# Attention and routed experts: a pair's loads in eight transfers behind exponentials, a batch's rows stored together

## The chip, the cores and the metric

The kernel runs on one core of a Trainium2 chip. The metric is the device time of one execution in microseconds (us): the median of three timed runs. The profile is of one further execution.

## The reference

Inputs are q, k, v of 8 batches, 8 heads, 576 positions and 64 values a head, and the weights of 8 experts. Cut to what matters:

```python
q_rot, k_rot = rotate(q), rotate(k)                  # x1*cos - x2*sin, x1*sin + x2*cos
scores = matmul(q_rot, k_rot.T) / sqrt(64)
attn = softmax(scores)
x = matmul(attn, v)                                  # -> 4608 tokens of 512 values
e_idx = argmax(x @ w_gate)                           # one expert per token
gate = softmax(x @ w_gate)[e_idx] * sigmoid(x @ w_output_gate)[e_idx]
out = gate * (relu(x @ w1[e_idx]) @ w2[e_idx])
```

## The kernel before

**The tiling.** Two heads make a pair, so there are 4 pairs a batch and 32 in all. A pair's scores are computed in nine units of 128 x 576 (128 rows of one head, and one unit of what is left of both). The schedule is counted in steps, nine to a pair, one for each unit: `step` (L367) writes the instructions of a unit, or of two units at a time, and behind them whatever is listed for the step. `PREPARED`, `EVENTS` and `PREP` (L45 to L59) list (name, step relative to the pair's first, order within the step). The program is unrolled and has one order of instructions for each engine; an engine, and SP's queue of transfers too, takes its instructions in that order, and each waits for the data that it needs.

**A unit.** TensorE computes the scores (`sc`, L521); VectorE copies them out and takes their extreme (`pm`, L530); ScalarE takes the exponential with the sum of a row (L537, `exp` at L532); VectorE transposes blocks of 32 (`pt`, L543 and L545); and in the following pair's steps TensorE multiplies with v (`acc`, L567, `values` at L556), in 18 blocks of 32 keys, eight small matmuls each (four row groups by two heads). Then ScalarE evicts (`ac`, L574 to L576), TensorE turns the result back (L582), and VectorE divides by the sums into `xb` (L594).

**Preparation.** A pair needs q and k, each with a copy whose halves are swapped: four planes of 128 x 576 in the tile `raw` (two buffers). `load` (L452) brings them in two transfers of 576 KB on SP's queue: k's two planes at step -18, q's at step -15. POOL multiplies with the table of cosines and sines (L472), k first, adds (L476), ScalarE rounds to the high part (L482), POOL subtracts to get the low part (`kq`, L485). In POOL's order the next pair's k multiplication stands just ahead of this pair's low part. `loadv` (L458) brings v in two transfers of 576 KB, one a head, at steps 5 and 7 of the pair itself, into `v` (two buffers). None of these transfers waits for anything but its buffer: a load of q and k can go as soon as POOL has finished the pair two ahead, a load of v as soon as the values of the pair two ahead have been read.

**Ranking and storing.** After a batch's last pair, `place` (L607) lists the work of choosing experts, numbering tokens and storing the batch's rows of `xb` to memory, mostly on POOL, over the following pairs. A token's gate factor is copied into the rows by `gated` (L690) and the rows leave by `store` (L697), three transfers of 640, 640 and 160 KB on SP's queue. For the first six batches L812 lists them: columns 0 and 1 gated at 29, the first store at 33, the rest gated at 38, the other stores at 42 (in steps, counted from 20 steps behind the batch's last pair's start). The last two batches go another way.

**The experts.** When all of attention's steps are written, `body` (L221 to L231) lists the first weight loads (`wr`, L1098) on the same queue; ScalarE and VectorE split weights in two parts (L1107, L1109), and TensorE multiplies (L1142, L1150, L1192).

Of the kernel before, what the change touches and what calls it, by code (L numbers as in the profile page):

```python
# [14 lines left out]
AF = mybir.ActivationFunctionType  # L15
# [12 lines left out]
NCH = 5  # L28
# [13 lines left out]

NB, TAIL, PE_ = S // 32, 160, 192

PREPARED = [("load1", -18, 1), ("load0", -15, 1), ("mult1", -14, 1), ("mult0", -11, 1), ("add", -9, 1), ("hi", -6, 1), ("lo", -5, 2)]  # L45
EVENTS = [
    ("lasts", 1, 2), ("loadv0", 5, 2), ("loadv1", 7, 2),
    ("av0", 12, 1), ("av1", 13, 0), ("av2", 14, 0), ("av3", 16, 0),
    ("den0", 10, 2), ("den1", 15, 2), ("den2", 15, 3), ("evict", 16, 1), ("newxb", 18, 1), ("back", 19, 1), ("divide", 19, 2),
]  # L50
# [3 lines left out]
PREP = {  # L54
# [5 lines left out]
}  # L60

PIECES = ((0, 5), (5, 7), (7, 12), (12, 18))
# [69 lines left out]
class Small:  # L132


    def __init__(self, p):
        self.p, self.tag = p, "sc"
# [139 lines left out]
class Attention:  # L276


    def __init__(self, tc, nb, pools, cc, ident, ii, first, trib, oneb, cnt, zero, qk, v, xd, row, lists):
        nc = tc.nc  # L280
        px, px2, pa2, pp1, pp2, ps_s, small, ps_a = pools
        NT = nb * S
        own = []
        self.tops = px.tile([P, NCH, E + 1], F32, name="score"), px.tile([P, NCH + 1, E], BF16, name="hot")
        self.inits = [lambda t=t, x=x: nc.gpsimd.memset(t, x) for t, x in zip(self.tops, (0.5, 0.0))]

        def init(bd, z, rz, ac):
            nc.gpsimd.memset(ac[:, NCH - 1, :, :], 0.0)
            nc.gpsimd.tensor_copy(bd.rearrange("p a b -> p (a b)"), zero)
            nc.gpsimd.memset(z, 1.0)  # L290
            nc.gpsimd.memset(rz, 1.0)

        for i in range(2):
            o = (px.tile([P, 2, P], F32R, name=f"bd{i}"), px.tile([P, 2 * NCH], F32, name=f"z{i}"),
                 px.tile([P, 2 * NCH], F32, name=f"rz{i}"), pa2.tile([P, NCH, 4, 32], F32, tag=f"ac{i}", name=f"ac{i}", bufs=1))
            self.inits.append(lambda o=o: init(*o))
            own.append(o)
        npair = nb * NP
        self.G, self.pairs = 9 * npair, []
        raw0, rt = first  # L300
        for n in range(npair):
            self.pairs.append(Pair(tc, pools, n, own[n % 2], ident, ii, rt, qk[n // NP, n % NP], v[n // NP, n % NP]))
        self.pairs[0].raw = raw0

        self.todo = {}
        self.last, self.later = [], []
        at = self.at
        xbs = {}

        def newxb(b):  # L310
            xbs[b] = px2.tile([P, NCH, XW], F32, tag="xb", name=f"xb{b}")

        for i, pr in enumerate(self.pairs):
            g, b = 9 * i, i // NP
            fs = {"lasts": pr.lasts, "den0": pr.den0, "den1": pr.den1, "den2": pr.den2, "evict": pr.evict, "back": pr.back,
                  "newxb": lambda pr=pr, b=b: newxb(b) if pr.hp == 0 else None}
            fs["divide"] = lambda pr=pr, b=b: pr.divide(xbs[b])
            for t, n in ((slice(0, 1), "0"), (slice(1, 2), "1"), (slice(0, 2), "")):
                fs[f"mult{n}"] = lambda pr=pr, t=t: pr.mult("P", t)
                fs[f"add{n}"] = lambda pr=pr, t=t: pr.add("P", t)  # L320
                fs[f"hi{n}"] = lambda pr=pr, t=t: pr.high(t)
                fs[f"lo{n}"] = lambda pr=pr, t=t: pr.low("P", t)
            for t in range(2):
                fs[f"load{t}"] = lambda pr=pr, t=t: pr.load(t)
                fs[f"loadv{t}"] = lambda pr=pr, t=t: pr.loadv(t)
            for k, (b0, b1) in enumerate(PIECES):
                fs[f"av{k}"] = lambda pr=pr, b0=b0, b1=b1: [pr.values(j) for j in range(b0, b1)]
            for name, o, k in [*PREP.get(i, PREPARED), *EVENTS]:
                at(g + o, k, fs[name])
            if i % NP == NP - 1:  # L330
                fs = place(tc, (px, px2, small), self.pairs, b, NT, cc, trib, oneb, cnt, xbs, xd, row, lists, self.tops, self.later)
                if b == nb - 1:
                    self.last = fs
                else:
                    for k, p, f in fs:
                        at(g + PLACE + k, p, f)
# [5 lines left out]
    def at(self, g, k, f):  # L342
        self.todo.setdefault((g, k), []).append(f)
# [10 lines left out]
    def start(self, consts):  # L354
        at = self.at
        for f in self.inits:
            f()

        self.pairs[1].load(1)
        self.pairs[1].load(0)  # L360
        self.pairs[0].start()
        self.todo.setdefault((0, 0), []).insert(0, self.pairs[0].started)
        for g, f in consts:
            at(g, 2, f)
        self.rest(lambda g: g < 0)
# [36 lines left out]
class Pair:  # L402
# [46 lines left out]
    def eng(self, eng):  # L449
        return self.nc.gpsimd if eng == "P" else self.nc.vector  # L450

    def load(self, t):  # L452

        if t:
            self.raw = self.pp2.tile([P, 4, S], F32, tag="raw", name=f"raw{self.nm}")
        self.nc.sync.dma_start(out=self.raw[:, 2 * t:2 * t + 2, :], in_=self.qkd[:, 2 * t:2 * t + 2, :])

    def loadv(self, t):  # L458

        if t == 0:  # L460
            self.v = self.pa.tile([P, 2, NB, D], F32, tag="v", name=f"v{self.nm}")
        self.nc.sync.dma_start(out=self.v[:, t, :, :], in_=self.vd[:, t, :, :])


    def sides(self, a, t, s, x):
# [26 lines left out]
            self.nc.scalar.copy(self.bd[r, :, r], self.kq.bitcast(F32)[r, 0:2, QM:S])  # L492

    def begin(self):
        self.pc, self.ps, self.m = {}, {}, {}

        self.pt = self.pa.tile([P, 9, S], F32, tag="pt", name=f"pt{self.nm}")

# [33 lines left out]
    def exp(self, i):  # L532
        zi = 8
        if self.STEPS[i]:
            c, h = self.STEPS[i]
            zi = 2 * c + h
        self.nc.scalar.activation(self.pc[i], self.pc[i], AF.Exp, bias=self.m[i], scale=-1.0, accum_out=self.z[:, zi:zi + 1])  # L537

    def turn(self, units):

# [66 lines left out]
def place(tc, pools, pairs, b, NT, cc, trib, oneb, cnt, xbs, xd, row, lists, tops, later):  # L607
# [82 lines left out]
    def gated(c0, c1):  # L690

        V.tensor_copy(xbs[b][:, c0:c1, P], T["eg"][:, c0:c1])
# [115 lines left out]
    if b == NT // S - 2:  # L808
        later += [lambda i=i: store(i) for i in range(3)]
        fs += [(22, 2, s13)]  # L810
    else:
        fs += [(29, 2, lambda: gated(0, 2)), (33, 2, lambda: store(0)), (38, 2, lambda: gated(2, NCH)),  # L812
               (42, 2, lambda: store(1)), (42, 2, lambda: store(2))]
    return fs


# [523 lines left out]
```

## Time and profile before

| | us |
|---|---|
| median of 3 runs (961.87 to 965.65) | 965.22 |
| the profiled execution | 961.01 |
| its span, from first to last instruction | 959.2 |
| TensorE (PE) busy | 911.8 (95%) |
| VectorE (DVE) busy | 753.4 (79%) |
| ScalarE (ACT) busy | 658.7 (69%) |
| GpSimd (POOL) busy | 528.9 (55%) |

The span is the profiled execution's instructions; its own time has 1.8 us around it. PE is the matmuls and PEld the weight loads that overlap them. Attention takes the first half of the span, the experts the second. TensorE's granted clock is at full speed in all slices.

### The profile page before, as it was taken

Reading aid. Unit: us, or ns where it says so; the run is one execution under the profiler, and the core shown is the slowest. Engines: PE = TensorE matmul, PEld = TensorE weight load, DVE = VectorE, ACT = ScalarE, POOL = GpSimd, SP = SyncE. Lnnn points to the kernel's source line nnn. Section 1 sums busy time; section 2 is a strip of 40 time slices with the busy share of each in tenths; the row PEclk is TensorE's granted clock in tenths of the full one; section 3 lists DMA queues with packets and bytes.
Section 4 is the critical chain, followed back from the end, with each engine's and each line's share of the span. In section 5 each row is a group of like instructions: output and inputs, shape, how many; then the busy total and the mean of one; then the engine's idle time right before and its main releaser. Section 6 shows DMA issues by size and latency. Waiting matters only on the chain.

```text
span 959.2 us, 34178 instructions
## 1 busy us (share of the span) xinstructions
PE 911.8 (95%) x14445; PEld 789.2 (82%) x14445; DVE 753.4 (79%) x1354; ACT 658.7 (69%) x1373; POOL 528.9 (55%) x483
## 2 busy tenths in 40 slices
PE   4999999999999989989899999999999999999997
PEld 3777777878878777777788998999899998999986
DVE  6899999999999989989588776657765757668562
ACT  4777789899998988797764544457645656556562
POOL 5898898898989898797222222142514315042140
PEclk9999999999999999999999999999999999999999
DMA  6554466365636555554299867667876868768560
GB/s 239 199 180 147 178 227 231 142 227 200 245 135 243 203 182 182 177 186 173 97 359 313 304 205 239 219 217 270 290 269 226 292 199 303 255 225 289 198 203 25
DMA packets 57821, 208.42 MB, mean 217 GB/s; under 512 B 7818, under 2 KB 8252, under 8 KB 57664
## 3 DMA queue, kind: packets, MB, share of 16 engines
q1 hardware_dynamic: 49920, 183.78, 54.8%
q0 software_dynamic: 6464, 21.26, 5.9%
q8 instruction: 115, 1.88, 0.8%
q10 hardware_dynamic: 1280, 1.15, 0.4%
q14 instruction: 42, 0.34, 0.1%
HBM read 186.09 MB, written 22.43 MB: 217 GB/s over the span
## 4 chain that ended last, share of the span: by engine, by line
PE 69%; DVE 13%; issue 6%; POOL 5%; ACT 5%; DMA 2%; POOLq 0%; DVEq 0%; SPq 0%; ACTq 0%
PE py L1192 20%; PE ph L1150 19%; PE acc L567 12%; PE sc L521 10%; DVE pm L530 6%; PE ph L1142 3%; DVE pt L545 2%; ACT pm L537 2%; PE acc L582 2%; POOL raw L472 2%; DVE pt L543 2%; PE mtp L1115 2%; POOL kq L485 1%; DVE xb L594 1%; DMA out<-y,2idx 1%
## 5 line engine op out<-in xcount | busy, mean ns | idle before, releaser
L537 ACT ACTIVATE pm<-pm,m 128x576 f32<-128x576 f32 x288 | 221.7, 770 | 55.9 <-DVE pm L530 52.6
L1109 DVE TENSOR_TENSOR wl<-wr,wh 128x1024 fp32r<-128x1024 f32 x172 | 216.2, 1271 | 37.2 <-ACT wh L1107 34.2
L530 DVE TENSOR_SCALAR_CACHE_REDUCE pm<-sc 128x576 f32<-128x576 f32 x288 | 205.1, 744 | 24.4 <-PE sc L521 19.4
L567 PE MATMUL acc<-pt,v 32*64 32x128 f32 (+1 forms) x9216 | 198.5, 295 | 21.2 <-issue 9.2
L1192 PE MATMUL py<-wh,ht 128*128 128x512 f32 x640 | 214.0, 400 | 0.0
L1150 PE MATMUL ph<-xt,wh 128*128 128x256 f32 x1088 | 198.3, 284 | 0.0
L567 PEld LDWEIGHTS acc<-pt,v 32*64 32x64 f32 x9216 | 157.5, 131 | 47.6 <-issue 29.7
L1107 ACT CAST wh<-wr 128x1024 fp32r<-128x1024 f32 x184 | 187.8, 1049 | 0.0
L521 PE MATMUL sc<-kq 64*128 64x288 f32 x1536 | 159.8, 320 | 15.4 <-ACT kq L482 9.6
L1150 PEld LDWEIGHTS ph<-xt,wh 128*128 128x128 f32 x1088 | 169.8, 190 | 2.6 <-DVE xt L1131 1.2
L472 POOL TENSOR_TENSOR raw<-raw,rt 128x1152 f32<-128x1152 f32 x62 | 164.8, 2658 | 0.0
L521 PEld LDWEIGHTS sc<-kq 64*128 64x128 f32 x1536 | 121.5, 190 | 48.7 <-issue 20.8
L1150 PE MATMUL ph<-xt,wl 128*128 128x256 f32 x544 | 154.0, 283 | 0.0
L1192 PEld LDWEIGHTS py<-wh,ht 128*128 128x128 f32 x640 | 120.3, 188 | 25.2
L1192 PE MATMUL py<-wl,ht 128*128 128x512 f32 x320 | 125.8, 393 | 0.0
L543 DVE STREAM_TRANSPOSE pt<-pm 128x576 f32<-128x576 f32 x160 | 116.7, 759 | 2.1 <-ACT pm L537 2.1
L1166 ACT ACTIVATE ht<-ph 128x512 fp32r<-128x512 f32 x68 | 40.7, 598 | 112.9 <-PE ph L1150 103.3
L1197 POOL DMA_INDIRECT out<-y,2idx x24 | 26.0, 1083 | 166.1 <-ACT y L1206 104.7
L1167 DVE SCALAR_TENSOR_TENSOR ht<-ph,ht 128x512 fp32r<-128x512 f32 x68 | 47.0, 691 | 73.7 <-ACT ht L1166 70.3
L1150 PEld LDWEIGHTS ph<-xt,wl 128*128 128x128 f32 x544 | 103.0, 189 | 0.2 <-DVE wl L1109 0.2
L545 DVE STREAM_TRANSPOSE pt<-pm 128x1152 f32<-128x1152 f32 x64 | 87.9, 1373 | 0.7 <-ACT pm L537 0.7
L485 POOL TENSOR_TENSOR kq<-raw,kq 128x1152 fp32r<-128x1152 f32 (+1 forms) x33 | 82.8, 2509 | 8.7 <-ACT kq L482 8.5
(243 smaller groups left out, 1105.0 us busy)
## 6 DMA issues: line engine op xcount, KB each, us to landing
wr<-in_w SPq DMA_DIRECT2D x184, 512.0 KB, 4.4
raw<-in_qk SPq DMA_DIRECT2D x64, 576.0 KB, 5.2
v<-in_v SPq DMA_DIRECT2D x64, 576.0 KB, 6.1
xd<-xb SPq DMA_DIRECT2D x16, 640.0 KB
xd<-xb SPq DMA_DIRECT2D x8, 160.0 KB, 5.1
rt<-in_rope ACTq DMA_DIRECT2D x1, 576.0 KB
xg<-xd,2idx POOLq DMA_INDIRECT x24, 6.7
out<-y,2idx POOLq DMA_INDIRECT x24, 3.4
```

The source lines that it names most:

```text
L472: self.eng(eng).tensor_tensor(out=rv, in0=rv, in1=rt, op=ALU.mult)
L485: self.eng(eng).tensor_tensor(out=self.sides(self.kq, t, 0, x), in0=self.sides(self.raw, t, 0, x), in1=self.sides(self.kq.bitcast(F32), t, ...
L521: self.nc.tensor.matmul(self.ps[i][:, a, :HS], st, self.kq[r, mov, x], start=(n == 0), stop=(n == 2))
L530: self.nc.vector.tensor_scalar(self.halves(i), self.ps[i][:, :, :HS], 1.0, FAR, op0=ALU.mult, op1=ALU.min, accum_out=self.m[i])
L537: self.nc.scalar.activation(self.pc[i], self.pc[i], AF.Exp, bias=self.m[i], scale=-1.0, accum_out=self.z[:, zi:zi + 1])
L543: self.nc.vector.transpose(out=self.pt[:, c + 5 * h, :], in_=self.pc[units[0]])
L545: self.nc.vector.transpose(out=self.pt[:, c:c + 6:5, :], in_=self.pc[units])
L567: nc.tensor.matmul(self.acc[h * D:h * D + D, a, o:o + 32 * n], self.v[r, h, j, :], self.pt[r, u:u + n, 32 * j:32 * j + 32], start=(j == 0) ...
L1107: self.nc.scalar.copy(wh, r)
L1109: eng.tensor_tensor(out=wl, in0=r, in1=wh.bitcast(F32), op=ALU.subtract)
L1150: nc.tensor.matmul(ph[:, f, :], st[:, dc, fs], mv[:, dc, :], start=(n == 0), stop=(n == 11))
L1192: self.nc.tensor.matmul(py[h], st[:, f, hs], mv, start=(f == 0 and n == 0), stop=(f == 7 and n == 2))
```

## The change

Each of q's and k's four planes gets a transfer of its own (288 KB), at steps -18 to -15, in the order k, k swapped, q, q swapped; v is loaded in four quarters at steps 4 to 7. Each transfer is made dependent on the exponential of one unit: q and k of a pair on those of units 0 to 3 of the pair two ahead, v on those of units 4 to 7 of the same pair. Pair 1's loads, at the program's start, depend on none. For the first six batches the gate factors are copied at once at 24, and all three stores are listed at 33.

```diff
-PREPARED = [("load1", -18, 1), ("load0", -15, 1), ("mult1", -14, 1), ("mult0", -11, 1), ("add", -9, 1), ("hi", -6, 1), ("lo", -5, 2)]
+LOADED = [(f"load{t}", t - 18, 2) for t in range(4)]
+
+PREPARED = [*LOADED, ("mult1", -14, 1), ("mult0", -11, 1), ("add", -9, 1), ("hi", -6, 1), ("lo", -5, 2)]
 EVENTS = [
-    ("lasts", 1, 2), ("loadv0", 5, 2), ("loadv1", 7, 2),
+    ("lasts", 1, 2), *[(f"loadv{t}", t + 4, 2) for t in range(4)],
...
-            for t in range(2):
-                fs[f"load{t}"] = lambda pr=pr, t=t: pr.load(t)
-                fs[f"loadv{t}"] = lambda pr=pr, t=t: pr.loadv(t)
+            for t in range(4):
+                fs[f"load{t}"] = lambda i=i, pr=pr, t=t: pr.load(t, self.pairs[i - 2].ex[t])
+                fs[f"loadv{t}"] = lambda pr=pr, t=t: pr.loadv(t, pr.ex[t + 4])
...
-        self.pairs[1].load(1)
-        self.pairs[1].load(0)
+        for t in range(4):
+            self.pairs[1].load(t)
...
-    def load(self, t):
-
-        if t:
+    def behind(self, dma, ex):
+
+        if ex is not None:
+            info = mybir.DependencyInfo(mybir.DependencyClass.Sync, mybir.DependencyReason.DATA)
+            self.tc.add_manual_dep(dma.ins, ex.ins.name, info, reason="transfers evenly in time")
+
+    def load(self, t, ex=None):
+
+        if t == 0:
             self.raw = self.pp2.tile([P, 4, S], F32, tag="raw", name=f"raw{self.nm}")
-        self.nc.sync.dma_start(out=self.raw[:, 2 * t:2 * t + 2, :], in_=self.qkd[:, 2 * t:2 * t + 2, :])
-
-    def loadv(self, t):
+        t ^= 2
+        self.behind(self.nc.sync.dma_start(out=self.raw[:, t, :], in_=self.qkd[:, t, :]), ex)
+
+    def loadv(self, t, ex):
 
         if t == 0:
             self.v = self.pa.tile([P, 2, NB, D], F32, tag="v", name=f"v{self.nm}")
-        self.nc.sync.dma_start(out=self.v[:, t, :, :], in_=self.vd[:, t, :, :])
+        h, j = t // 2, slice(t % 2 * 9, t % 2 * 9 + 9)
+        self.behind(self.nc.sync.dma_start(out=self.v[:, h, j, :], in_=self.vd[:, h, j, :]), ex)
...
-        self.nc.scalar.activation(self.pc[i], self.pc[i], AF.Exp, bias=self.m[i], scale=-1.0, accum_out=self.z[:, zi:zi + 1])
+        self.ex[i] = self.nc.scalar.activation(self.pc[i], self.pc[i], AF.Exp, bias=self.m[i], scale=-1.0, accum_out=self.z[:, zi:zi + 1])
...
-        fs += [(29, 2, lambda: gated(0, 2)), (33, 2, lambda: store(0)), (38, 2, lambda: gated(2, NCH)),
-               (42, 2, lambda: store(1)), (42, 2, lambda: store(2))]
+        fs += [(24, 2, s13), (33, 2, lambda: store(0)), (33, 2, lambda: store(1)), (33, 2, lambda: store(2))]
```

The same `LOADED` takes the place of the two loads in `PREP`'s lists for pairs 2 and 3.

## Rows read from the trace of the kernel before

**Rows 1.** The page: busy us (share), instructions by engine; a queue: packets, MB, share

```profile
PE 911.8 (95%) x14445; PEld 789.2 (82%) x14445; DVE 753.4 (79%) x1354; ACT 658.7 (69%) x1373; POOL 528.9 (55%) x483
...
q8 instruction: 115, 1.88, 0.8%
```

**Rows 2.** Stretch of attention: length, busy time by engine, PEclk, DMA share, GB/s

```profile
core 0: us, PE busy (x) PEld busy (x) DVE busy (x) ACT busy (x) POOL busy (x), PEclk, DMA share, GB/s
13.30:472.80 459.50, 428.33 (x11323) 353.19 (x11322) 428.13 (x888) 386.81 (x1000) 394.90 (x372) 1.00 0.54 191
```

**Rows 3.** The chain of waits through one pair: start us, us, what

```profile
82.79 1.41 DVE pm L530 x4
...
96.18 1.40 DVE pm L530 x3
```

**Rows 4.** Timeline of SP's queue: start us, us of issue, transfer

```profile
340.31 1.81 SPq L456 DMA_DIRECT2D raw<-in_qk  x2
342.22 0.85 SPq L462 DMA_DIRECT2D v<-in_v  x2
...
351.27 0.38 SPq L700 DMA_DIRECT2D xd<-xb  x1
353.88 0.92 SPq L456 DMA_DIRECT2D raw<-in_qk  x2
357.98 0.81 SPq L462 DMA_DIRECT2D v<-in_v  x2
...
447.99 65.19 SPq L1098 DMA_DIRECT2D wr<-in_w  x25
```

**Rows 5.** Timeline of PEld: start us, us, operation, count [idle before <- releaser]

```profile
144.44 0.43 PEld L521 LDWEIGHTS sc<-kq 64*128 64x128 f32 x5 [0.77 <-issue]
...
351.80 1.02 PEld L567 LDWEIGHTS acc<-pt,v 32*64 32x64 f32 x56 [1.15 <-issue]
353.05 0.82 PEld L521 LDWEIGHTS sc<-kq 64*128 64x128 f32 x12 [0.23 <-issue]
354.04 1.04 PEld L567 LDWEIGHTS acc<-pt,v 32*64 32x64 f32 x60 [0.17 <-issue]
356.92 0.74 PEld L567 LDWEIGHTS acc<-pt,v 32*64 32x64 f32 x36 [1.84 <-issue]
...
372.50 0.20 PEld L567 LDWEIGHTS acc<-pt,v 32*64 32x64 f32 x5 [1.53 <-issue]
...
412.99 1.30 PEld L567 LDWEIGHTS acc<-pt,v 32*64 32x64 f32 x73 [1.72 <-issue]
...
417.55 1.01 PEld L567 LDWEIGHTS acc<-pt,v 32*64 32x64 f32 x53 [1.31 <-issue]
```

**Rows 6.** Stretches of a burst of loads and of a wait (columns as in rows 2)

```profile
69.00:71.00 2.00, 1.92 (x18) 1.51 (x14) 2.00 (x6) 1.96 (x7) 2.00 (x2) 1.00 1.00 385
...
348.00:351.00 3.00, 2.86 (x69) 1.96 (x68) 2.76 (x5) 2.94 (x7) 3.00 (x2) 1.00 0.36 137
351.00:352.00 1.00, 0.20 (x11) 0.20 (x19) 1.00 (x5) 1.00 (x2) 1.00 (x3) 1.00 0.00 0
```

**Rows 7.** Line 567: waits in the weight loads' queue, ns min/median/max

```profile
L567 PEldq EVENT_SEMAPHORE  x33: 51/51/1509, 28.3 to 461.4; - x33
```

**Rows 8.** Timeline of ACT: the end of unit 1's exponential in pair 14

```profile
208.36 0.19 ACT L537 ACTIVATION_READ_ACCUMULATOR pm<-pm,m 128x1 f32 x1
```

**Rows 9.** Timeline of POOL: pair 16's k multiplication, pair 15's low part

```profile
208.70 2.66 POOL L472 TENSOR_TENSOR raw<-raw,rt 128x1152 f32<-128x1152 f32 x1
...
212.06 2.65 POOL L485 TENSOR_TENSOR kq<-raw,kq 128x1152 fp32r<-128x1152 f32 x1
```

**Rows 10.** Timeline of PEld: pair 15's first scores

```profile
217.64 0.83 PEld L521 LDWEIGHTS sc<-kq 64*128 64x128 f32 x12 [0.22 <-issue]
```

**Rows 11.** Tile wr: its 512 KB loads from issue to landing

```profile
DMA to landing us min/median/max: 3.4/4.4/7.2
```

**Rows 12.** Timeline of ACT: unit 7 of the last pair, the first split of weights

```profile
460.02 0.19 ACT L537 ACTIVATION_READ_ACCUMULATOR pm<-pm,m 128x1 f32 x1
...
468.33 2.95 ACT L1107 CAST wh<-wr 128x1024 fp32r<-128x1024 f32 x3
```

More of the change, by code (lines that the diff above doesn't have):

```diff
@@ L56 @@
     1: (("mult1", -9, 1), ("add1", -9, 1), ("mult0", -8, 1), ("add0", -7, 1), ("hi1", -5, 1), ("lo1", -4, 1), ("hi0", -3, 1), ("lo0", -2, 1)),
[1 row of a table removed]
+    2: (*LOADED, ("mult1", -11, 1), ("add1", -10, 1), ("mult0", -9, 1), ("add0", -7, 1), ("hi1", -6, 1),
         ("lo1", -5, 1), ("hi0", -4, 1), ("lo0", -3, 1)),
[1 row of a table removed]
+    3: (*LOADED, ("mult1", -11, 1), ("mult0", -9, 1), ("add", -7, 1), ("hi", -4, 1), ("lo", -4, 2)),
 }
@@ L494, in begin @@
     def begin(self):
-        self.pc, self.ps, self.m = {}, {}, {}
+        self.pc, self.ps, self.m, self.ex = {}, {}, {}, {}
         self.pt = self.pa.tile([P, 9, S], F32, tag="pt", name=f"pt{self.nm}")
```

2 rows, old and new, of the table PREP are left out of this document.

## The prediction

> **What bounds the kernel now.** I began with the stretches. Attention runs from 13.3 to 472.8 us, and in it TensorE (428.3 us) and VectorE (428.1 us) are busy for equal shares of 459.5 us [rows 2]: neither has room. The change edits only loads and stores of this half; the experts behind it stream weights through code that it leaves alone. The chain of waits then shows what a quiet pair costs: its last scores are read by VectorE at 82.79 and those of the next pair at 96.18, so 13.39 us a pair, by matmuls and VectorE work that follow on each other without a gap [rows 3]. 32 such pairs would take 428 us; the stage is about 30 us longer, part of it the batches' own ranking work and the start.
>
> Next I looked for where a pair is longer. SP's queue shows it: the loads of v are issued as soon as a pair's values have been read, and from 342.22 to 357.98 they stand 15.76 us apart instead of 13.39 [rows 4]. The weight-load rows of those stretches show why. Before the loads at 351.80, 356.92, 372.50, 412.99 and 417.55 TensorE sat idle for 1.15, 1.84, 1.53, 1.72 and 1.31 us, and for 0.77 us before 144.44, each time "issue", that is, no other engine was waited for; the same change of line costs 0.16 to 0.23 us elsewhere, as at 353.05 and 354.04 [rows 5].
>
> What is missing there is the program itself. From the idle time at 351.80 to the one at 356.92 lie 56 + 12 + 60 = 128 weight loads [rows 5], and as many matmuls. The page counts 14445 of each, 28890 in all, and 115 packets of kind "instruction" with 1.88 MB, 16 KB each: 251 instructions a packet [rows 1]. So the two waits are one packet apart, at its edges: TensorE had run dry before its next block came. And the block came late behind loads. Two transfers of q and k at 340.31 and two of v at 342.22, 576 KB each, keep the transfer engines moving until about 350; in 351 to 352 they move nothing at all (share 0.00) while TensorE still waits [rows 4, 6]. The block thus passed no earlier than the end of the burst. The next wait follows a 640 KB store at 351.27 and two loads at 353.88 [rows 4].
>
> **The change, part by part.** (1) Loads. A pair's four transfers of 576 KB become eight of 288 KB, each allowed only after one exponential: q and k behind units 0 to 3 two pairs ahead, v behind units 4 to 7 of the pair itself. A transfer of 288 KB takes 0.77 us at the 385 GB/s of a burst [rows 6], and units are 13.39 / 9 = 1.5 us apart, so no queue builds up. The six waits lose all but the ordinary 0.2 us: 0.57 + 0.95 + 1.64 + 1.33 + 1.52 + 1.11 = **-7.1 us**. They lie on TensorE in a stage without slack, so I count them whole. The Trainium skill, Runtime: NRT & Kernel Launch, Instruction fetch mechanics, says that the engine fetches its next block of 256 instructions while it executes the current one, at a cost that is mostly hidden. The trace agrees on the size of the block, not on the cost, which is 7.1 us here; by that sentence this term would be about 0 and the sum 4 us above the time before.
>
> (2) What is late next: transfers are now under way in every phase of a pair, 8 x 0.77 / 13.39 = 46% of the time, also where TensorE goes through a block fastest (128 weight loads from 351.80 to about 355.1, in 3.3 us [rows 5]). A block behind one slice waits 0.77 / 2 = 0.38 us on average. One such block in each of 28 pairs gives at most 28 x 0.46 x 0.38 = 4.9 us, at least 0. I take **+1.5**, nearer to zero, because most bursts of before, three times as deep, were survived: only six waits stand out.
>
> (3) The gate on POOL. POOL multiplies the k half as soon as it is there, and the previous pair's low part (L485), which that pair's scores need, stands behind this multiplication in POOL's order. Today nothing gates it: in the tightest kind of pair, one a batch, it starts at 208.70 and the low part at 212.06 [rows 9]. After the change the second slice waits for unit 1, whose exponential is read out at 208.36 + 0.19 = 208.55 [rows 8]. From issue to landing no row shows 288 KB; 512 KB take 3.4 / 4.4 / 7.2 us (least, median, most) [rows 11], less the 0.6 us of the missing bytes 2.8 / 3.8 / 6.6. I take 3.0, near the least, since little else is then in flight: ready at 211.55, the low part done at 211.55 + 2.66 + 0.70 (two small steps between them) + 2.65 = 217.56, and the scores start at 217.64 [rows 9, 10]. That fits by 0.08 us. Bounds for 7 batches: 0, and 7 x 0.7 = 5 us at 3.8. I take **+0.5**. What POOL loses there it has back in its later waits for ScalarE.
>
> (4) SP's queue. Everything in it now stands behind exponentials, the stores and the first weights too. The last v slice waits for unit 7 of the last pair, read out at 460.2 [rows 12], so the first weights, issued at 447.99 today [rows 4], go after 461. They are first read at 468.33, three in 2.95 us [rows 12]; landing in 4.4 us makes some 465.6 for the first [rows 11], and 1.36 us more for each of the following. It fits, but TensorE's blocks then meet a denser burst than before. Bounds 0 and 4 us (first weights landing 7.2 us after issue, and one more late block); I take **+0.8**.
>
> (5) Stores. Six batches store 640 + 640 + 160 KB at the end of one pair, not over two. Gating in one POOL copy instead of two saves some 0.2 us of POOL; the factors are then ready. The stores are 3.8 us of transfers at 385 GB/s [rows 6] in front of the next pair's first slices, which land about 1 us later, and POOL's multiplication with them. Bounds 0 and 6 x 0.5; I take **+1.0**. The store's buffer is free a pair earlier; no row shows a wait for it today, so that brings nothing.
>
> (6) Finer tiles need about two more waits of TensorE's queue per pair, at 51 ns a piece [rows 7]: 32 x 2 x 0.051 = 3.3 us at most, 0 at least. The queue runs ahead of the array, so **+0.3**.
>
> Sum: -7.1 + 1.5 + 0.5 + 0.8 + 1.0 + 0.3 = -3.0 us. The profiled execution took 961.0 us (span 959.2), so 958.0. It is the fastest one shown; the median, 965.22, is 4.2 us above it. Late blocks are a matter of phase and the likeliest thing to differ between executions of one program, so I let half of the 4.2 go as well: 958.0 + 2.1, about **960 us**, 0.54% under the median.
>
> **The rivals.** *Given back* (0.20): the long waits vanish and short ones take their place in each pair, as in (2) at its upper bound, with (6) at 1.3. That is -7.1 + 4.9 + 0.5 + 0.8 + 1.0 + 1.3 = +1.4 against the profile's 961.0; with half of the 4.2 us, 964.5. For it speaks that a fast block has only 3.3 us [rows 5]; against it, that bursts three times as deep rarely hurt.
>
> *Nothing hangs on the bursts* (0.12): the late blocks have another cause, and time stays at 965. The position after whole bursts [rows 4, 6] speaks against it. The Trainium skill, DMA: Bandwidth & Descriptors, Queues, rings and completion order, has each engine go round between its queues packet by packet; by that a block would never wait for a burst to drain, and spreading the loads would bring nothing. The trace disagrees: at 351 to 352 the burst had drained and TensorE still stood.
>
> *POOL gate, the slower side* (0.18): slices land later than 3.0 us after issue, because the refills or the stores are in front of them. Each us beyond costs a us in each of 7 batches, on TensorE itself. It decides from about 3.5 us, where 7 x 0.42 eats the 3 us won. At the median-like 3.8, together with the stores' 1 us, the scores wait 1.7 us a batch: 7 x 1.7 = 12, in place of the 1.5 of (3) and (5), so 970.5. For it: a margin of 0.08 us. Against: in most other pairs POOL multiplies later by itself.
>
> **How the numbers follow.** Main case 0.50, from 953 to 963 as the bounds of (2) to (6) make it; some 0.44 of it lies under 960.4. Within 0.5% (4.8 us, about what a measurement of this kernel can tell from no change) lie the rest of it, 0.06, and the two middle rivals, 0.32: 0.38. Slower by more than that: 0.18. The range runs from 952 to 970; left out are the worse half of the gate's cases and a larger gain.
>
> **What would show it.** Right: SP's rows have one load per 1.5 us; idle times of over 0.8 us before values (L567) are gone between 340 and 420; v loads stay about 13.4 us apart there. (2) is wrong if there are many new "issue" waits of 0.3 to 0.8 us. The gate shows as TensorE's scores waiting for POOL L485, and the raw load as POOL's releaser. (4) shows as ScalarE L1107 waiting for weights near 468. The forecast falls if waits of over 1 us stay although no burst is left, or if scores wait for POOL in most pairs.

## The result and the profile after

The changed kernel took **975.04 us** (median of 4 runs, 971.85 to 978.39), the kernel before 963.55 beside it (4 runs, 957.19 to 965.65): 1.0136 times as long, 95% interval 1.0107 to 1.0166. Here and below, the ratio and its interval are worked out from the fast runs and need not equal the quotient of the two medians. It is slower by more than the range allowed. The profiled execution took 974.82 us, its span is 973.0.

The page of the changed kernel. First the busy times and the refills of the instruction queue, which answer to [rows 1], then POOL's multiplication (busy, mean ns | idle before it and what ended it), and the issues (KB each, median us from issue to landing):

```profile
PE 921.5 (95%) x14445; PEld 795.9 (82%) x14445; DVE 755.0 (78%) x1354; ACT 659.4 (68%) x1373; POOL 529.5 (54%) x477
...
q8 instruction: 115, 1.88, 0.8%
...
L482 POOL TENSOR_TENSOR raw<-raw,rt 128x1152 f32<-128x1152 f32 x62 | 164.4, 2653 | 31.9 <-DMA raw<-in_qk 31.9
...
raw<-in_qk SPq DMA_DIRECT2D x124, 288.0 KB, 3.0
```

and the multiplication's line in the page of the kernel before:

```profile
L472 POOL TENSOR_TENSOR raw<-raw,rt 128x1152 f32<-128x1152 f32 x62 | 164.8, 2658 | 0.0
```

The programs are equally long (115 refills, the same instructions on TensorE). What is new is 31.9 us in which POOL stands in front of its multiplications and waits for q and k; before, that number was 0.0. The landing of 3.0 us that the prediction took is the true median of these 124 transfers. It is not what the pairs behind the stores got.

**Where the time lies.** ScalarE's rows give the place of the last pair's unit 7, to be laid beside 460.02 in [rows 12]; the two earlier ones are unit 0 and unit 1 of the pair shown further down.

```profile
196.70 0.19 ACT L547 ACTIVATION_READ_ACCUMULATOR pm<-pm,m 128x1 f32 x1
...
197.46 0.19 ACT L547 ACTIVATION_READ_ACCUMULATOR pm<-pm,m 128x1 f32 x1
...
472.48 0.19 ACT L547 ACTIVATION_READ_ACCUMULATOR pm<-pm,m 128x1 f32 x1
```

Attention up to there is 472.48 - 460.02 = 12.5 us longer; the rest of the span grew from 499.2 to 500.5 us, by 1.3. TensorE's lines up to that point say in what. Before (busy us, mean ns | idle before them, and what ended it):

```profile
L567 PE MATMUL acc<-pt,v 32*64 32x160 f32 (+1 forms) x8928 | 192.0, 295 | 18.5 <-DVE xb L594 8.0 <-issue 6.5 <-ACT rc L720 3.9
L521 PE MATMUL sc<-kq 64*128 64x288 f32 x1524 | 157.8, 319 | 5.8 <-DVE pm L530 3.5 <-issue 1.0 <-POOL kq L485 0.6
L582 PE MATMUL acc<-ii,ac 128*128 128x160 f32 x300 | 48.8, 309 | 1.5 <-ACT ac L576 0.2
```

and after:

```profile
L577 PE MATMUL acc<-pt,v 32*64 32x128 f32 (+1 forms) x8928 | 192.4, 295 | 13.8 <-DVE xb L604 7.1 <-ACT rc L730 4.0 <-issue 2.3
L531 PE MATMUL sc<-kq 64*128 64x288 f32 x1524 | 163.7, 322 | 11.9 <-POOL kq L495 6.0 <-DVE pm L540 4.3 <-issue 0.6
L592 PE MATMUL acc<-ii,ac 128*128 128x160 f32 x300 | 52.3, 324 | 2.3 <-ACT ac L586 1.5
```

The late instruction blocks did go: "issue" in front of the values fell from 6.5 to 2.3 us. In their place scores wait for POOL's low part: 6.0 us, where it was 0.6. And the same matmuls take longer: 5.9 us more for the scores, 3.5 for the turning back. In all, TensorE up to that point is busy 10.2 us longer (429.6 in place of 419.3 us) and idle 2.2 us longer. The waits of attention with its end (0 to 490 us; total, times, longest) complete the picture:

```profile
POOL raw L482 <- DMA raw<-in_qk: 31.9, 17, 4.5
...
DVE pm L540 <- PE sc L531: 26.3, 34, 2.8
...
PEld sc L531 <- POOL kq L495: 7.5, 7, 2.0
```

VectorE, as full as TensorE, waits for scores 26.3 us in place of 19.4.

**One batch of it.** SP's queue, at the end of the first pair behind a batch:

```profile
193.90 0.90 SPq L710 DMA_DIRECT2D xd<-xb  x2
194.85 1.40 SPq L712 DMA_DIRECT2D xd<-xb  x1
196.95 3.32 SPq L465 DMA_DIRECT2D raw<-in_qk  x4
```

The three stores go just ahead of the four slices. The first slice leaves as soon as unit 0 is read out (196.70 + 0.19), the second behind unit 1 (197.46 + 0.19 = 197.65). The stretches there (columns as in [rows 2]), and, below them, three stretches to come back to:

```profile
194.00:196.00 2.00, 1.95 (x18) 1.56 (x14) 2.00 (x6) 1.93 (x7) 1.92 (x2) 1.00 0.82 182
196.00:198.00 2.00, 1.55 (x42) 1.29 (x45) 2.00 (x3) 1.99 (x8) 1.58 (x2) 1.00 0.98 386
198.00:200.00 2.00, 2.00 (x75) 1.71 (x57) 2.00 (x5) 1.98 (x6) 1.28 (x3) 1.00 1.03 387
200.00:202.00 2.00, 2.00 (x46) 1.51 (x44) 1.88 (x4) 1.83 (x4) 0.00 (x0) 1.00 0.96 346
202.00:203.60 1.60, 1.60 (x83) 1.34 (x80) 1.56 (x5) 1.23 (x3) 0.00 (x0) 1.00 0.96 324
...
324.30:327.70 3.40, 3.40 (x16) 3.07 (x18) 2.67 (x6) 2.34 (x8) 3.32 (x2) 0.50 0.21 40
382.30:385.70 3.40, 3.40 (x17) 3.12 (x18) 1.84 (x5) 2.42 (x7) 3.32 (x3) 0.50 0.00 1
430.10:433.50 3.40, 3.40 (x16) 3.07 (x17) 2.33 (x6) 3.33 (x11) 3.40 (x2) 0.50 0.89 331
```

The engines are full from 196 to 203.6. From 194 on they move 364 + 772 + 774 + 692 + 518 = 3.1 MB (GB/s times us, slice by slice), which is more than the stores (1.47 MB) and all four slices (1.18 MB) together. So k's second slice was complete when nearly everything issued around it had been moved, and not after the stores' rest alone. The chain of waits and POOL's timeline show when (idle before in brackets):

```profile
197.69 5.84 DMA raw<-in_qk
...
203.66 2.65 POOL L482 TENSOR_TENSOR raw<-raw,rt 128x1152 f32<-128x1152 f32 x1 [4.23 <-DMA raw<-in_qk]
206.26 2.64 POOL L495 TENSOR_TENSOR kq<-raw,kq 128x1152 fp32r<-128x1152 f32 x1
```

and TensorE's weight loads who pays:

```profile
208.96 0.70 PEld L531 LDWEIGHTS sc<-kq 64*128 64x128 f32 x10 [2.03 <-POOL kq L495]
```

The chain has one link of 5.84 us from unit 1 to the multiplication; in two more batches the same link is 5.12 us (at 312.70) and 6.01 us (at 370.82). In [rows 9] the low part stands right behind this multiplication; here the multiplication comes 4.23 us after POOL was ready.

**The clock.** In the three stretches listed last TensorE's granted clock is 0.50, its lower level of 1.2 GHz. Before, no stretch of attention up to the last pair was below full speed. Behind the last pair both kernels have one such stretch (the changed one from 481.3); the page's 40 slices are too coarse to show the one of the kernel before:

```profile
472.90:476.30 3.40, 3.40 (x16) 3.40 (x17) 0.15 (x2) 1.17 (x5) 0.00 (x0) 0.50 0.02 5
```

TensorE's rows at the first of the changed kernel's three, and the same ten matmuls of the last pair:

```profile
323.27 0.92 PE L531 MATMUL sc<-kq 64*128 64x288 f32 x10 [1.64 <-POOL kq L495]
324.12 2.93 PE L592 MATMUL acc<-ii,ac 128*128 128x160 f32 x10
...
473.56 1.62 PE L592 MATMUL acc<-ii,ac 128*128 128x160 f32 x10 [1.04 <-ACT ac L586]
```

It stood idle for 1.64 us, waiting for POOL, computed for about 1 us, and then ten matmuls that take 1.62 us at 473.56 took 2.93. The second stretch follows a wait for POOL too (0.95 us, at 382.26). The third does not: it follows 1.24 us of waiting for ScalarE's eviction (at 429.88), and experiment 5, whose scores are on time, has the same 1.24 us with the lower clock behind it (at 415.37). Nor does every wait bring the lower clock: the one of 2.03 us at 208.96 did not. Three times 3.4 us at half the clock is work of 5.1 us at full clock: 5.1 us lost, half of the 10.2 us by which TensorE's busy time grew up to 472.67. Of the 5.1 us, the 3.4 of two stretches go with the late scores. The Trainium skill, TensorE: Matmul & The Clock Gate, HAM oscillation, describes this: waits for transfers between pieces of work make the engine start the next piece at the lower clock. The trace agrees in kind, though its waits of 0.95 to 1.64 us are shorter than those of the section's example. The other half of the growth can't be assigned: the ends of matmuls are modelled.

### The profile page after: what moved, and what is told of

Its sections match the earlier page's. It is cut to its first block, busy times and chain, and to the rows that moved or that the text cites. A ratio compares the mean times of both kernels' runs of the same rounds, so it can differ in the third digit from the quotient of the medians.

```text
span 973.0 us, 34540 instructions
## 1 busy us (share of the span) xinstructions
PE 921.5 (95%) x14445; PEld 795.9 (82%) x14445; DVE 755.0 (78%) x1354; ACT 659.4 (68%) x1373; POOL 529.5 (54%) x477
## 4 chain that ended last, share of the span: by engine, by line
PE 68%; DVE 12%; ACT 7%; issue 5%; POOL 4%; DMA 4%; POOLq 0%; DVEq 0%; ACTq 0%
PE py L1201 21%; PE ph L1159 19%; PE acc L577 11%; PE sc L531 9%; DVE pm L540 6%; ACT pm L547 3%; PE ph L1151 3%; DMA raw<-in_qk 2%; PE acc L592 2%; DVE pt L555 2%; PE mtp L1124 2%; POOL kq L495 2%; DVE pt L553 2%; POOL raw L482 2%; DVE xb L604 1%
## 5 line engine op out<-in xcount | busy, mean ns | idle before, releaser
L540 DVE TENSOR_SCALAR_CACHE_REDUCE pm<-sc 128x576 f32<-128x576 f32 x288 | 205.5, 746 | 32.1 <-PE sc L531 26.3
L531 PE MATMUL sc<-kq 64*128 64x288 f32 x1536 | 165.8, 324 | 21.7 <-ACT kq L492 9.8
L482 POOL TENSOR_TENSOR raw<-raw,rt 128x1152 f32<-128x1152 f32 x62 | 164.4, 2653 | 31.9 <-DMA raw<-in_qk 31.9
L531 PEld LDWEIGHTS sc<-kq 64*128 64x128 f32 x1536 | 124.5, 192 | 58.3 <-issue 20.8
L1206 POOL DMA_INDIRECT out<-y,2idx x24 | 28.1, 1172 | 166.8 <-ACT y L1215 103.6
```

Of the source, the lines that this page charges most:

```text
L482: self.eng(eng).tensor_tensor(out=rv, in0=rv, in1=rt, op=ALU.mult)
L531: self.nc.tensor.matmul(self.ps[i][:, a, :HS], st, self.kq[r, mov, x], start=(n == 0), stop=(n == 2))
L540: self.nc.vector.tensor_scalar(self.halves(i), self.ps[i][:, :, :HS], 1.0, FAR, op0=ALU.mult, op1=ALU.min, accum_out=self.m[i])
```

## The experiments

Theory **A**: the stores in one row stand in front of the next pair's first slices, these come too late for POOL, and with it come late scores. **B**: the exponentials themselves make the slices late, in every pair. **C**: eight small transfers make or keep TensorE's instruction blocks late. Diffs are against the changed kernel unless another is named. A time "against" another is the median beside that of the kernel before, run next to it, with the ratio and its 95% interval. Where the expectations name runs, e5 is experiment 5 and e10 is experiment 9.

**1. The stores of before, on the new loads**

```diff
-        fs += [(24, 2, s13), (33, 2, lambda: store(0)), (33, 2, lambda: store(1)), (33, 2, lambda: store(2))]
+        fs += [(29, 2, lambda: gated(0, 2)), (33, 2, lambda: store(0)), (38, 2, lambda: gated(2, NCH)),
+               (42, 2, lambda: store(1)), (42, 2, lambda: store(2))]
```

> The changed kernel with the stores where they were (gated at 29 and 38, stored at 33 and 42); the eight gated loads stay. Theory A (three stores in a row stand in front of the next pair's first slices, so POOL's k multiplication and the scores behind it start late, once a batch): the delay is halved and shared by two pairs, of which one has room, so most of the loss goes: 964 to 968 us, and TensorE waits for POOL L495 a third as long as the changed kernel's 13.5 us. Theory B (the exponentials themselves make the slices late in every pair): 972 us or more. Theory C (eight smaller transfers keep TensorE's instruction blocks late): no change from 975.

987.75 us (984.3 to 994.22) against 959.42: 1.0284 [1.0254, 1.0313]. By the number this is B's "972 or more", but the waits up to 480 us name something that no theory had:

```profile
PEld acc L577 <- DVE xb L604: 27.8, 17, 5.6
...
DVE xb L604 <- DMA xd<-xb: 16.7, 5, 4.8
```

VectorE's division, which writes a batch's rows, waits five times for a store that has not yet read the buffer, and the values behind it wait for the division. Scores wait for POOL only 0.4 us here. In a queue in which every load stands behind an exponential, stores listed at 42 leave so late that they hold up the buffer of the batch two ahead. So the two halves of the change belong together, and this run doesn't price the stores.

**2. The stores behind k's slices, ahead of v's**

```diff
-(33, 2, lambda: store(0)), (33, 2, lambda: store(1)), (33, 2, lambda: store(2))
+(37, 2, lambda: store(0)), (37, 2, lambda: store(1)), (37, 2, lambda: store(2))
```

> The changed kernel with all three stores listed four steps later (37), so that they stand behind the next pair's four slices of q and k and ahead of its slices of v. Theory A: the slices land 3 us after their issue in every pair, POOL's waits for them of over 2 us are gone, scores wait under 3 us in all for POOL, and TensorE's late blocks stay away: 959 to 963 us, below the kernel before. Theory B: 972 or more. Theory C: 975.

967.22 us (966.36 to 967.87) against 959.42: 1.0079 [1.0058, 1.0099], so 0.6% of the 1.4% go; that lies between A's 959 to 963 and B's 972. The waits:

```profile
POOL raw L482 <- DMA raw<-in_qk: 28.2, 20, 2.7
...
DVE fx L674 <- POOL score L671: 3.5, 4, 1.5
```

Scores now wait for POOL by 0.2 us in all, as A expected. On SP's queue the stores stand behind three slices, and q's last goes behind them. POOL still waits 28.2 us for slices: by 2.66 us at 75.14 and 1.89 at 102.00, before any store has left, by 1.3 to 2.1 us for k's slices behind the first five batches (1.5 in the mean), where the changed kernel has 3.6 to 4.5 (4.1), and there by 1.4 to 2.6 us for q's last slice. POOL's timeline and the chain in one batch:

```profile
199.53 2.67 POOL L482 TENSOR_TENSOR raw<-raw,rt 128x1152 f32<-128x1152 f32 x1 [1.31 <-DMA raw<-in_qk]
```

```profile
200.66 6.12 DMA raw<-in_qk
```

Unit 1 is read out at 196.29 here, so POOL has k 3.2 us later, and no longer 6.0; now q's last slice, behind the stores, takes 6.1. So B is right in that the gates alone make POOL wait, but that alone costs the scores next to nothing; in the changed kernel the stores add some 2.6 us to it. What is left of the loss hangs, in part, on q's slice: POOL's ranking steps stand behind its multiplication, and VectorE, which takes its instructions in order, waits for one of them. TensorE's clock fell twice before the end of attention (at 271.7, behind such a wait, and at 439.0).

**3. The slices of q and k wait for no exponential**

```diff
-pr.load(t, self.pairs[i - 2].ex[t])
+pr.load(t)
```

> The changed kernel with the waits of the q and k slices taken away; those of v stay. Since SP's queue goes in order, the slices go right behind the last v slice of the pair before and, once a batch, behind the three stores. Theory A: the stores are still in front, the first slices gain at most the 1 to 2 us by which unit 1 is later than the end of the stores' issue: 969 to 974. Theory B: the gate is gone, POOL starts as early as before: 960 to 964.

971.58 us (970.05 to 974.4) against 959.42: 1.0127 [1.0097, 1.0157]. As A expected: POOL waits for slices only 9 times in place of 17, but still 28.3 us and by up to 4.6, and scores for POOL 6.5 us. Freed of their own gates, the slices still stand behind the stores, and those behind v's gated slices.

**4. No transfer waits for an exponential**

```diff
-        if ex is not None:
+        if False:
```

> The changed kernel with no transfer waiting for an exponential; eight transfers a pair and the stores in one place stay. The queue runs ahead as in the kernel before, so the stores leave earlier than the slices that POOL needs next. Theory A and B: about the kernel before, 961 to 966, with TensorE's waits for late blocks of 0.8 to 1.8 us back. Theory C: stays at 970 or more.

967.97 us (965.33 to 971.39) against 959.42: 1.0093 [1.0059, 1.0128]. Now POOL waits for no slice, and scores for POOL by 0.3 us once; yet the time is just above A's and B's 961 to 966. What comes back is what the change had removed. TensorE's values up to the last pair:

```profile
L577 PE MATMUL acc<-pt,v 32*64 32x160 f32 (+1 forms) x8928 | 196.4, 299 | 21.8 <-issue 9.7 <-DVE xb L604 8.0 <-ACT rc L730 3.9
```

"issue" is 9.7 us, where the changed kernel has 2.3 and the kernel before 6.5. Three of these waits (1.98, 2.29 and 1.79 us, at 301.86, 360.34 and 421.18) have TensorE's lower clock behind them, for 13.6 us in all, so 6.8 us lost. The two together are 10.0 us, where attention up to the last pair is 8.4 us longer than before. So the gates do what the prediction said of them, and size alone (288 KB) does nothing for the instruction blocks.

**5. All transfers four units earlier**

```diff
+AHEAD = [(f"load{t}", t - 22, 2) for t in range(4)]
...
-PREPARED = [*LOADED,
+PREPARED = [*AHEAD,
...
-*[(f"loadv{t}", t + 4, 2) for t in range(4)]
+*[(f"loadv{t}", t, 2) for t in range(4)]
...
-pr.load(t, self.pairs[i - 2].ex[t])
+pr.load(t, self.pairs[0].ex[t] if i == 2 else self.pairs[i - 3].ex[t + 5])
-pr.loadv(t, pr.ex[t + 4])
+pr.loadv(t, pr.ex[t])
```

> The changed kernel with every transfer four units earlier: q and k behind units 5 to 8 of the pair three ahead, v behind units 0 to 3 of its own pair; sizes, number and order of the transfers and the stores' place stay. Theory A (the slices come too late for POOL, which sets scores and, in VectorE's order, the batch's reductions): POOL's waits for q and k fall from 31.9 us to under 5, scores no longer wait for the low part, 956 to 961 us. Theory C (transfers in every phase make TensorE's blocks late): as the changed kernel or 1 to 3 us below it, 970 to 975.

958.31 us (955.82 to 961.9) against 961.6: 0.999 [0.9961, 1.002]. The same eight gated transfers, the same stores in a row, and the whole loss is gone: POOL waits for no slice, scores for POOL 0.8 us, and up to the last pair "issue" in front of the values is 0.7 us. C falls with it. The gates are not the fault, their place is. There is no gain either. The longest wait for an instruction block, 3.5 us, now stands at the end of attention (it ends at 469.28), behind a stretch in which the first weights and gathers fill the transfer engines (share 1.01 from 463 to 465); the lower clock follows there, and once more at 415.5.

**6. The same, with the stores in the gap between the gates**

```diff
 (experiment 5, and)
-(33, 2, lambda: store(0)), (33, 2, lambda: store(1)), (33, 2, lambda: store(2))
+(38, 2, lambda: store(0)), (38, 2, lambda: store(1)), (38, 2, lambda: store(2))
```

> The same, with the stores behind unit 4 of the next pair, between v's slices and those of q and k. Theory A: no transfer that POOL needs soon stands behind a store, 955 to 960 us; what is left over the kernel before can only be late blocks behind the 1440 KB of stores. Theory C: 970 or more.

964.79 us (961.0 to 966.1) against 961.6: 1.0035 [0.9997, 1.0072]. That is a little above A's 955 to 960, and its interval still holds 1. POOL waits for slices by 0.6 us only, but four blocks are late, 7.2 us in all and by up to 2.7, and TensorE's clock fell three times in attention. The same 1440 KB in one row, listed at 33 in experiment 5, made no block that late up to the last pair; why their place matters so much is not shown.

**7. The kernel before with the new stores alone**

```diff
 (against the kernel before)
-        fs += [(29, 2, lambda: gated(0, 2)), (33, 2, lambda: store(0)), (38, 2, lambda: gated(2, NCH)),
-               (42, 2, lambda: store(1)), (42, 2, lambda: store(2))]
+        fs += [(24, 2, s13), (33, 2, lambda: store(0)), (33, 2, lambda: store(1)), (33, 2, lambda: store(2))]
```

> The kernel before with only the stores' part of the change: gated in one at 24, all three at 33; loads of 576 KB that wait for nothing. The queue runs ahead, so the stores go as soon as their rows are ready. Theory A: no wait of POOL, so the stores by themselves cost nothing but a late block now and then: 957 to 964 us. If the stores are what costs wherever they stand: 968 or more.

963.40 us (958.52 to 968.42) against 961.6: 1.0041 [1.0007, 1.0074]. The stores alone cost 0.4%, of the 1.4%; "issue" in front of the values rises to 10.4 us in 14 waits, and no score waits for POOL. For late scores it takes gates and stores together.

**8. Four gated transfers of 576 KB**

```diff
-LOADED = [(f"load{t}", t - 18, 2) for t in range(4)]
+LOADED = [(f"load{t}", 2 * t - 17, 2) for t in range(2)]
...
-pr.load(t, self.pairs[i - 2].ex[t])
+pr.load(t, self.pairs[i - 2].ex[2 * t + 1])
-pr.loadv(t, pr.ex[t + 4])
+pr.loadv(t, pr.ex[2 * t + 5])
...
-        t ^= 2
-        self.behind(self.nc.sync.dma_start(out=self.raw[:, t, :], in_=self.qkd[:, t, :]), ex)
+        t = slice(2 - 2 * t, 4 - 2 * t)
+        self.behind(self.nc.sync.dma_start(out=self.raw[:, t, :], in_=self.qkd[:, t, :]), ex)
```

(and the like for v)

> The changed kernel with four transfers of 576 KB instead of eight of 288: k behind unit 1, q behind unit 3 of the pair two ahead, v behind units 5 and 7; stores as in the change. Theory A (lateness of the gate, not the splitting): k lands 0.5 to 1 us later than its two slices do, so as slow as the changed kernel or slower, 975 to 982. If the eight small transfers themselves are what costs: 962 to 968.

979.04 us (976.36 to 981.32) against 961.6: 1.0217 [1.0151, 1.0283]. POOL's wait for slices grows to 47.0 us in 19 waits: fewer and larger transfers behind the same gates are worse, since the whole 576 KB must land after unit 1. That speaks against C once more. The late blocks are back too, with 7.5 us of "issue" up to the last pair: with experiment 4, it takes gates and small transfers together to remove them.

**9. Only k's slices earlier, by two steps**

```diff
+AHEAD = [(f"load{t}", t - (20 if t < 2 else 18), 2) for t in range(4)]
...
-PREPARED = [*LOADED,
+PREPARED = [*AHEAD,
...
-pr.load(t, self.pairs[i - 2].ex[t])
+pr.load(t, self.pairs[i - 3].ex[t + 7] if t < 2 and i > 2 else self.pairs[i - 2].ex[t])
```

> The changed kernel with only k's two slices two steps earlier, behind units 7 and 8 of the pair three ahead; q's slices, v's and the stores as in the change. Theory A: POOL multiplies k first, and only that multiplication stands in front of the previous pair's low part, so scores stop waiting for POOL's low part and most of the loss goes: 960 to 966 us; the slices of q land late as before, with little harm, and TensorE's blocks behind the stores may be late once a batch. If q's slices or the stores themselves were what costs, the time stays at 970 or more. Theory B: 970 or more, since q's slices stay behind the exponentials.

971.2 us (970.55 to 975.32) against 961.15: 1.0101 [1.008, 1.0122]. A miss, and SP's queue in one batch shows that the edit was not what I had meant:

```profile
194.07 0.38 SPq L466 DMA_DIRECT2D raw<-in_qk  x1
194.55 1.81 SPq L711 DMA_DIRECT2D xd<-xb  x2
196.41 1.15 SPq L713 DMA_DIRECT2D xd<-xb  x1
197.65 2.78 SPq L466 DMA_DIRECT2D raw<-in_qk  x3
```

One slice of k went ahead of the stores, the second still behind them, at 197.65, and POOL needs both:

```profile
202.88 2.66 POOL L483 TENSOR_TENSOR raw<-raw,rt 128x1152 f32<-128x1152 f32 x1 [3.27 <-DMA raw<-in_qk]
```

It starts 5.2 us after the second slice's issue. (The profiled execution is the slowest of the four.)

**10. Both slices of k ahead of the stores**

```diff
 (experiment 9, with)
-t - (20 if t < 2 else 18)
+t - (21 if t < 2 else 18)
-self.pairs[i - 3].ex[t + 7]
+self.pairs[i - 3].ex[t + 6]
```

> The changed kernel with both slices of k three steps earlier, behind units 6 and 7 of the pair three ahead, so that both are issued in front of the batch's stores (in e10 the second of them was issued behind the stores, so POOL still waited); q's slices, v's and the stores as in the change. Theory A: POOL's multiplication of k finds its slices there also behind the stores, scores wait for POOL's low part by under 0.5 us, and what is left of the loss is q's slices landing late, late instruction blocks behind the stores and half-clock stretches: 962 to 968 us. If the time stays at 970 or more, it is not k's slices but q's, or the stores in themselves, that carry the loss.

961.26 us (960.02 to 964.88) against 962.53: 0.9999 [0.9977, 1.0022]. That is just under A's 962 to 968. One step more than in experiment 9 for two transfers of 288 KB, and the loss is gone; the stores, and q's and v's slices with their gates, stand as in the change. The waits up to 490 us:

```profile
POOL raw L483 <- DMA raw<-in_qk: 10.4, 10, 3.6
...
PE sc L532 <- POOL kq L496: 0.5, 1, 0.5
```

POOL still waits (at 198.51 by 0.68 us for k's slices, at 205.11 by 1.12 for q's), and nobody behind it pays: scores wait for POOL 0.5 us. SP's queue and POOL in one batch show what the two slices gained:

```profile
192.26 0.42 SPq L466 DMA_DIRECT2D raw<-in_qk  x1
192.77 2.37 SPq L711 DMA_DIRECT2D xd<-xb  x2
...
198.51 2.65 POOL L483 TENSOR_TENSOR raw<-raw,rt 128x1152 f32<-128x1152 f32 x1 [0.68 <-DMA raw<-in_qk]
```

k's second slice is issued ahead of the stores, at 192.26, and POOL still gets it only 6.2 us later, no sooner than a slice behind them. So a place ahead of the stores in the queue did not make the landing shorter; the earlier gate gave it the time. The last pair's unit 7 is read out at 458.29, 1.7 us before the place in [rows 12].

**11. The stores in five pieces, all loads as in the change**

```diff
+    def piece(c):
+        r, n = b * S + c * P, P if c < 4 else QR
+        nc.sync.dma_start(out=xd[r:r + n, :], in_=xbs[b][0:n, c, :])
...
-        fs += [(24, 2, s13), (33, 2, lambda: store(0)), (33, 2, lambda: store(1)), (33, 2, lambda: store(2))]
+        fs += [(24, 2, s13)] + [(27 + 2 * c, 2, lambda c=c: piece(c)) for c in range(5)]
```

> The changed kernel with each batch's rows stored in five transfers (four of 256 KB, one smaller) at steps 27, 29, 31, 33 and 35, all loads as in the change. Theory A: no more than 256 KB of stores stands in front of a pair's first slice, 0.7 us of transfers instead of 3.8, so POOL waits for k's slices by 1 us at most and the scores by under 0.5 us; late instruction blocks are gone: 958 to 964 us. Theory B (the exponentials themselves make the slices late, with or without stores): 968 or more, and POOL still waits for raw slices in each batch.

971.53 us (964.78 to 975.72) against 962.53: 1.0093 [1.0064, 1.0122]. A, as I had stated it, misses here: 958 to 964 was expected. (A piece is 320 KB; the 256 of the expectation left out the rows' further columns.) Between k's two slices stands one piece,

```profile
195.89 0.33 SPq L465 DMA_DIRECT2D raw<-in_qk  x1
196.27 0.46 SPq L716 DMA_DIRECT2D xd<-xb  x1
196.82 2.37 SPq L465 DMA_DIRECT2D raw<-in_qk  x3
```

and POOL still gets them 5 us after the second issue:

```profile
201.85 2.65 POOL L482 TENSOR_TENSOR raw<-raw,rt 128x1152 f32<-128x1152 f32 x1 [3.48 <-DMA raw<-in_qk]
```

though the transfer engines are not full behind that issue (busy shares of 0.56 and 0.84 from 196 to 198 and from 198 to 200). It is thus not only 1440 KB in one row that make k's second slice late; with a single store of 320 KB in front of it it was late as well, in a pair without a margin. What holds it up while the engines have room is not shown. By the number this is B's "968 or more", and POOL still waits for slices; but experiment 2 has POOL's waits without the scores' loss. The profiled execution is the slowest of the ten and is not the median's: a part of its time is one block that comes 4.1 us late behind the last pair (484.57), with the lower clock for 6.8 us.

**12. Experiments 5 and 11 together**

> The changed kernel with all its transfers four units earlier, as in e5, and each batch's rows stored in five transfers (four of 256 KB, one smaller) at steps 27, 29, 31, 33 and 35 instead of 640 + 640 + 160 KB at 33. Theory A (stores in one row stand in front of the slices and of TensorE's instruction blocks behind them): no deep burst is left in attention, so POOL waits for no raw slice, scores wait for no low part, no instruction block is late by over 1 us in attention; 953 to 957 us, 0.4 to 0.9% under the kernel before. Theory B (the exponentials themselves make slices late): above 965. Theory C (many small transfers keep the blocks late): as e5 or above, 958 to 962, with issue waits of 0.3 to 1 us spread over the pairs.

**956.18 us** (955.25 to 957.89) against 961.15: 0.9951 [0.9934, 0.9968], faster than both kernels, inside A's 953 to 957, and the only run with its interval below 1. From its waits up to 490 us:

```profile
PE acc L578 <- issue: 3.3, 5, 2.1
```

The "issue" waits are at 3.3 us where the kernel before has 9.2 (up to the last pair 0.8 where it has 6.5); the longest, 2.1, stands behind the last pair. No stretch of attention is below full clock, nor is the one behind the last pair, which cost the kernel before 1.7 us, and TensorE's busy time is the least of all: 910.5 us.

## Why the prediction was wrong

**Step (1), the late instruction blocks: right in kind.** Up to the last pair, "issue" in front of the values fell by 4.2 us, where (1) and (2) together had 5.6. Experiment 4 ties this to the gates: without them, with everything else as changed, the blocks are late again. By the Trainium skill, Runtime: NRT & Kernel Launch, Instruction fetch mechanics, a crossing into the next block is mostly hidden; the traces differ, with 6.5 us up to the last pair before, 9.7 in experiment 4 and 0.8 in experiment 12, so here its cost goes with how the transfers are laid.

**Step (3), the gate on POOL: right by itself.** It set the landing of k's second slice at 3.0 us after issue, "near the least, since little else is then in flight", and found a margin of 0.08 us. Experiment 2, which keeps the gates and has no store in front of k's slices, agrees: 3.2 us in the batch shown, and scores that wait for POOL by 0.2 us in all. But in six of the seven tight pairs of the changed kernel the stores are in flight, and there "little else" does not hold.

**Step (5), the stores: here it failed.** The prediction gives no working for "land about 1 us later". It should have been some 2.8 (5.84 in place of 3.0; 5.12 and 6.01 in two more batches), and its bound of 0.5 us a batch was no bound. Even 1 us later, against the 0.08 us that (3) had left, would have cost the scores 0.9 us a batch and 5.5 us in six, where (5) took 1.0. Shown: a wait of 2.03 us on TensorE in that batch; 6 to 7 such waits in all, 7.5 us in the weight loads' queue. I had treated (3) and (5) apart although they fall on the same slice of the same pair; only the rival added them. That rival, "POOL gate, the slower side", is what happened: 1.7 us a batch was forecast, up to 2.03 measured, 1.1 in the mean. That its 12 us for seven batches is close to the 12.5 us by which attention grew is luck: the scores' waits of 6 to 7.5 us are largely made up for by the 4.2 us of late blocks that went, so that TensorE is idle only 2.2 us longer; the other 10.2 us are its busy time, of which 5.1 us are the lower clock, a price that no step had. Experiment 10 shows the cause from the other side: with k's two slices three units earlier, and nothing else changed, 1.4% become 0.

**Step (4), the end of attention: right.** +0.8 forecast, +1.3 measured behind the last pair, where TensorE's longest wait for a block, 2.6 us, now stands. **Step (6)** can't be told apart from the rest. **The offset:** half of the 4.2 us between profile and median was let go; the kernel before has 963.55 beside the changed one, so this was right.

**What stays open.** Why k's second slice is complete only when nearly everything issued around it has been moved, rather than in its turn, is not settled. Experiment 10, with a slice as late in front of the stores as behind them, speaks against the queue's order as the reason; how the engines share their time is in no row. Open too are the other half of the growth of TensorE's busy time, and what decides whether the clock falls behind a wait.

## What to carry to other kernels

A gate that spreads transfers evenly is worth what it saves only if it stands early enough that the slowest landing, not the median one, still meets its reader; here three steps for two of eight transfers decided 1.4%. Where a wait is added to a queue, look for the reader with the smallest margin and then for everything else that crosses the same queue at that moment, and add the two up. Cutting the large stores up and laying them in the gaps gave the best time here, once the loads had margin; without the margin this bought little.

## What was not expected of the hardware

- TensorE's clock, at 1.00 up to the last pair before, fell to 0.50 for stretches of 3.4 us after idle times of 0.95 to 1.64 us (at 382.26, 429.88 and 323.27) in work that is otherwise dense: a short wait cost up to 1.7 us more than itself. The waits of up to 1.84 us of [rows 5], and one of 2.03 us in the changed kernel, did not.
- A transfer of 288 KB landed in 3.0 us at the median, and in 5 to 6 with stores around it (5.12, 5.84 and 6.01 us in three batches); issued ahead of the stores, in experiment 10, it reached its reader no sooner (6.2 us).
